# Fused attention, MoE and expert MoE: the experts' first pass in another order, and copies of MoE1's second product moved to ScalarE

## The chip, the core and the metric

The kernel runs on one core of a Trainium2 chip. Five engines run side by side, each with its own queue in program order: TensorE (PE; its weight loads are shown as PEld), VectorE (DVE), ScalarE (ACT), GpSimd (POOL) and SyncE (SP), which here only issues DMAs. GpSimd issues the indirect DMAs (gather and scatter by a list of rows) and ScalarE the stores of `y`. The metric is the device time of one execution in microseconds; lower is better.

## The reference

```python
attn_out = _attn_ref(q, k, v)                  # causal attention, 2 x 12 heads, 448 tokens, 64 wide
x = attn_out.transpose(0, 2, 1, 3).reshape(896, 768)
h = x @ w_in                                   # MoE1: 768 -> 2048
x = (h * (1 / (1 + exp(-1.702 * h)))) @ w_out  # 2048 -> 768
logits = x @ w_gate                            # MoE2: 8 experts, one per token
e_idx = argmax(logits, axis=1)
gate_w = softmax(logits)[e_idx]
eom = sigmoid(x @ w_output_gate)
for e in range(8):                             # 768 -> 1024 -> 768
    mask = e_idx == e
    out[mask] = gate_w[mask] * eom[mask, e] * (relu(x[mask] @ w1[e]) @ w2[e])
```

Everything is float32 to the outside.

## The kernel before

The kernel works with float32 products made of three: each operand is split into a high part (rounded, on ScalarE) and the rest (a subtraction, on VectorE or GpSimd), and TensorE adds high by high, high by rest and rest by high in PSUM. The order of all engines is written out by hand.

**Attention and MoE1's first product** take the first 246 us and are not touched.

**MoE1's second product** (`l2`) goes through the seven tiles of 128 tokens twice: first for the last 256 of the 768 columns (part "B"), then for the first 512 (part "A"). Within a tile it runs over 16 blocks of 128 rows of the weight (`kk`). Every fourth block it calls `gsplit`, which casts a piece of `g` on ScalarE (L505) and subtracts on GpSimd or VectorE (L507). After each block the weight stream is pumped: a weight tile is unpacked in three instructions on VectorE (L219, L221, L224), cast on ScalarE (L226) and subtracted on GpSimd (L228). At the end of a tile ScalarE copies the result out of PSUM (`y`, L597) and stores it. One tile behind, in hooks at given `kk`, the routing runs: `tr_y` transposes `y` on TensorE (L615) and copies the transposes to `yT` (L617), `logits` multiplies them with the gates (L627) and copies them out (L629, L632, L633); in part A follow `pick` (which expert, and the token's weight; L649 to L664) and `place` (the token's place in its expert's list, L670 to L677, and a scatter of token number and weight to the list in DRAM, L678).

**The experts** (`block`) are worked through in passes of up to 128 tokens; twelve passes run here, the first two both for expert 0. The first takes tokens of the first five tiles, so that it can start before the last tile is routed. A pass has twelve steps u. Steps 0 to 5 (`l1`, L875 and L879) multiply the tokens `xh`, `xl` with two blocks of `w1`; after steps 2 and 5 comes a relu on ScalarE (L883); `tr` transposes the hidden values (L889) and splits them into `hh`, `hl` (L891, L892). Steps 6 to 11 (`l2m`, L899 and L901) multiply with `w2`. After every step, `split` casts one later weight tile on ScalarE (L300) and subtracts on VectorE (L301), into one of six pairs `ent`; five tiles are split ahead during the last tile of part A. From split 12 on (counted from 0), each issues a load of the weights two passes ahead on SP's queue (`again`, `load32`, L272), which waits until the split has read its place; there are 24 places.

In the first pass, hooks `(hf, k)` between the matmuls of steps 0 to 5 and hooks `u` behind the later steps finish the routing of the last tile: `tr_y`, `logits`, `pick`, `place`, then `rest_lists` reads the rest of expert 0's list (`le0`, L724) and the other lists, `first_x` gathers its tokens into `xw` (L686) and `prep` transposes (L696) and splits (L698, L699) them for the second pass.

Of the kernel before, what the change touches and what calls it, by code (L numbers as in the profile page):

```python
# [9 lines left out]
F32 = mybir.dt.float32  # L10
# [97 lines left out]
def kernel(ctx, tc, q, k, v, w_in, w_out, w_gate, w_og, w1, w2, out):  # L108
    nc = tc.nc
# [3 lines left out]
    NE, _, F2 = w1.shape  # L113
# [7 lines left out]
    TT = NT // 128  # L121
# [25 lines left out]
    dram = ctx.enter_context(tc.tile_pool(name="dram", bufs=1, space=DRAM))  # L147
# [11 lines left out]
    with tc.manual_schedule():  # L159
# [90 lines left out]
        NR, NU, NENT = 24, 12, 6  # L250
# [23 lines left out]
        def again(o, u, last):  # L274


            if last and o + 2 < NE + 2:
                load32(o + 2, u)
# [13 lines left out]
        def split():  # L292
            if nsplit[0] == len(order):
                return
            p, u = order[nsplit[0]]
            hi, lo = entry_of[p, u] = entries[nsplit[0] % NENT]
            nsplit[0] += 1
            o, last = passes[p]
            raw = places[(NU * o + u) % NR]
            nc.scalar.copy(hi, raw)  # L300
            nc.vector.tensor_sub(lo, raw, hi.bitcast(F32))  # L301
            again(o, u, last)
# [155 lines left out]
        for s in range(len(steps) + LAG + AV_AT[-1]):  # L458
# [12 lines left out]
            for c in range(NKC):  # L471
                u = s - LAG - (NQ - 1) - AV_AT[c]
# [37 lines left out]
        for fq in range(4):  # L510
            for fc in range(4):
# [13 lines left out]
                if f == 15:  # L525
# [4 lines left out]
                    lgB = mp.tile([64, TT, 128], F32, name="lgB")  # L530
# [79 lines left out]
        def tr_y(t, part):  # L610
            n = 4 if part == "A" else 2
            y = ys_t.pop((t, part))
            p = ps.tile([128, 4, 128], F32, name="ps_yT", tag="tp", bufs=2)
            for c in range(n):
                nc.tensor.transpose(p[:, c], y[:, c * 128:(c + 1) * 128], ident)  # L615
            yT = mp.tile([128, 4, 128], F32, name="yT", tag="yT", bufs=1)
            nc.vector.tensor_copy(yT[:, :n], p[:, :n])  # L617
            yT_t[t, part] = yT

        lg_t = {}  # L620
# [1 line left out]
        def logits(t, part):  # L622
            n, k0 = (4, 0) if part == "A" else (2, 4)
            yT = yT_t.pop((t, part))
            p = ps.tile([128, 128], F32, name="ps_lT", tag="sm", bufs=2)
            for c in range(n):
                nc.tensor.matmul(p[32 * c:32 * c + 32], wg[:, k0 + c], yT[:, c], start=True, stop=True)  # L627
            if part == "B":
                nc.vector.tensor_copy(lgB[:, t], p[0:64])  # L629
            else:  # L630
                lT = mp.tile([128, 128], F32, name="lT", tag="lT", bufs=2)
                nc.vector.tensor_add(lT[0:64], p[0:64], lgB[:, t])  # L632
                nc.vector.tensor_copy(lT[64:128], p[64:128])  # L633
                lg_t[t] = lT

        def logits_sum(t):
            lg = ps.tile([128, 2 * NE], F32, name="ps_lg", tag="sm", bufs=2)
            nc.tensor.matmul(lg, lg_t.pop(t), esum, start=True, stop=True)
            lg_t[t] = lg

        ohs = {}

        def pick(t):
            logits_sum(t)
            lg = lg_t.pop(t)
            nm = mp.tile([128, 8], F32, name="nm", tag="nm", bufs=2)
            tmp = mp.tile([128, 3, NE], F32, name="tmp", tag="tmp", bufs=2)
            ohb = mp.tile([128, NE], BF16, name="ohb", tag="ohb", bufs=2)
            nc.vector.tensor_reduce(nm[:, 0:1], lg[:, 0:NE], axis=AX.X, op=ALU.max)  # L649
            nc.vector.scalar_tensor_tensor(tmp[:, 0], lg[:, 0:NE], nm[:, 0:1], rev,  # L650
                                           op0=ALU.is_equal, op1=ALU.mult)
            nc.vector.tensor_reduce(nm[:, 1:2], tmp[:, 0], axis=AX.X, op=ALU.max)
            nc.vector.tensor_scalar(ohb, rev, nm[:, 1:2], None, op0=ALU.is_equal)
            nc.vector.tensor_add(acc[t + 1], acc[t], ohb)
            nc.vector.tensor_scalar(nm[:, 2:3], nm[:, 0:1], -1.0, None, op0=ALU.mult)
            nc.scalar.activation(tmp[:, 1], lg[:, 0:NE], AF.Exp, bias=nm[:, 2:3], scale=1.0,
                                 accum_out=nm[:, 4:5])
            nc.vector.tensor_mul(tmp[:, 2], lg[:, NE:2 * NE], ohb)
            nc.vector.tensor_reduce(nm[:, 3:4], tmp[:, 2], axis=AX.X, op=ALU.add)
            nc.scalar.activation(nm[:, 5:6], nm[:, 3:4], AF.Exp, scale=-1.0)  # L660
            nc.vector.tensor_scalar_add(nm[:, 4:5], nm[:, 4:5], 1e-9)
            nc.vector.tensor_scalar_add(nm[:, 5:6], nm[:, 5:6], 1.0)
            nc.vector.tensor_mul(nm[:, 6:7], nm[:, 4:5], nm[:, 5:6])
            nc.vector.reciprocal(lst[:, t, 1:2], nm[:, 6:7])  # L664
            ohs[t] = ohb

        def place(t):
            ohb = ohs.pop(t)
            p = ps.tile([128, 2 * NE], F32, name="ps_rk", tag="sm", bufs=2)
            nc.tensor.matmul(p[:, 0:NE], sut, ohb, start=True, stop=False)  # L670
            nc.tensor.matmul(p[:, 0:NE], ones, acc[t], start=False, stop=True)
            tmp = mp.tile([128, NE], F32, name="tmp2", tag="tmp2", bufs=2)
            pos = mp.tile([128, 1], F32, name="pos", tag="pos", bufs=2)
            pos_i = mp.tile([128, 1], I32, name="pos_i", tag="pos_i", bufs=2)
            nc.vector.tensor_mul(tmp, p[:, 0:NE], ohb)
            nc.vector.tensor_reduce(pos, tmp, axis=AX.X, op=ALU.add)
            nc.vector.tensor_copy(pos_i, pos)  # L677
            nc.gpsimd.indirect_dma_start(  # L678
                out=xl_d[:, :], out_offset=bass.IndirectOffsetOnAxis(ap=pos_i.bitcast(U32), axis=0),
                in_=lst[:, t, :].bitcast(I32), in_offset=None, bounds_check=NT * NE - 1, oob_is_err=False)  # L680
# [4 lines left out]
        def gather(lw, xw, nrow=NT):  # L685
            nc.gpsimd.indirect_dma_start(  # L686
                out=xw, out_offset=None, in_=y1_d[0:nrow, :],
                in_offset=bass.IndirectOffsetOnAxis(ap=lw[:, 0:1].bitcast(U32), axis=0),
                bounds_check=nrow - 1, oob_is_err=False)

        def prep(xw):
            for hf in range(2):
                p = ps.tile([128, 4, 128], F32, name="ps_x", tag="tp", bufs=2)
                for c in range(3):
                    kk = 3 * hf + c
                    nc.tensor.transpose(p[:, c], xw[:, kk * 128:(kk + 1) * 128], ident)  # L696
                dst = xh[:, 3 * hf:3 * hf + 3]
                nc.scalar.copy(dst, p[:, 0:3])  # L698
                nc.vector.tensor_sub(xl[:, 3 * hf:3 * hf + 3], p[:, 0:3], dst.bitcast(F32))  # L699
# [30 lines left out]
        for t in range(TT):  # L730
            hooks = {}
# [6 lines left out]
        for t in range(TT):  # L738
# [13 lines left out]
            def h7(t=t):  # L752
                if t:
                    pick(t - 1)
# [13 lines left out]
            hooks = dict(zip(R_AT, (h2, h5, h7, h10, h15)))  # L768
# [7 lines left out]
        xw = xw_t[0]  # L776
# [78 lines left out]

        npass = [0]

        def block(lw, hooks):

            o, last = passes[npass[0]]  # L860
            p0 = npass[0]
# [4 lines left out]
            def hook(k):  # L866
                if k in hooks:
                    hooks[k]()
# [13 lines left out]
            def relu(hf):  # L882
                nc.scalar.activation(hs[:, hf * 512:(hf + 1) * 512], hps[hf], AF.Relu)  # L883
# [19 lines left out]
            for u in range(6):  # L903
                if u == 4:
                    tr(0)
                l1(u)
                if u % 3 == 2:
                    relu(u // 3)
                split()
            hook("b")  # L910
            pyA = ps.tile([128, 512], F32, name="ps_yA", tag="acc", bufs=4)
            pyB = ps.tile([128, 512], F32, name="ps_yB", tag="acc", bufs=4)
# [2 lines left out]
            for u in range(6, NU):  # L915
                g4, r = (u - 6) // 3 * 4, (u - 6) % 3
                if u == 7:
                    tr(1)
                if r < 2:
                    l2m(pyA, u, 512, range(g4 + 2 * r, g4 + 2 * r + 2))  # L920
                else:
                    l2m(pyB, u, 256, range(g4, g4 + 4))
                if u == 10:
                    nc.scalar.activation(ys[:, 0:512], pyA, AF.Copy, scale=scl)
                if u == 11:
                    nc.scalar.activation(ys[:, 512:768], pyB[:, 0:256], AF.Copy, scale=scl)
                split()
                hook(u)
            nc.gpsimd.indirect_dma_start(
                out=out[:, :], out_offset=bass.IndirectOffsetOnAxis(ap=lw[:, 0:1].bitcast(U32), axis=0),  # L930
# [2 lines left out]
        engs = (ET.PE, ET.DVE, ET.Pool, ET.Activation, ET.SP)  # L933
        lists = [lw0, le0] + [lwin[:, e] for e in ORDER[1:]] + lo_t

        def first_x():
            gather(le0, xw)

        block(lw0, {
            (0, 1): lambda: tr_y(TT - 1, "A"), (0, 2): last_logits, (0, 3): lambda: pick(TT - 1),  # L940
            (0, 5): last_place, (1, 0): rest_lists, (1, 3): first_x, (1, 4): counts, 6: further_constants,
            10: lambda: prep(xw)})
        nov = None

        def some(p):
# [65 lines left out]
```

## Time and profile before

| what | us |
|---|---|
| median of 3 runs | 633.17 |
| lowest and highest run | 633.08, 637.72 |
| the profiled execution | 635.76 |
| its span, first to last instruction | 634.0 |
| attention and MoE1's first product | 0 to 246 |
| second product, part B | 246 to about 307 |
| second product, part A | to about 394 |
| the experts' passes | 394 to 629 |

A line of the timeline holds the start, the time from the first to the last end of a run of equal instructions, the engine, the line of the kernel, the operation, output and input tile, the count, and in brackets how long the engine stood idle before and what it waited for. Instructions in a run overlap a little, so that a line's end is not always where the next begins.

### The profile page before, as it was taken

What the parts mean: (1) busy time and instruction counts of PE and PEld (TensorE: products, weight loads), DVE (VectorE), ACT (ScalarE), POOL (GpSimd) and SP (SyncE); (2) the same over time, 40 slices, a digit from 0 to 9 for tenths busy, and PEclk for the clock granted to TensorE, in tenths of its full rate; (3) what the DMA queues carried; (4) which work ended last, traced back from release to release, by engine and by line L of the source; (5) the groups of instructions that cost most, each with busy time, mean ns of one, the idle gap of its engine ahead of it and who ended that gap; (6) DMA issues with size and microseconds to landing.
All of it is one profiled execution on the core that took longest, in us unless ns stands there. A gap on an engine that the chain in (4) does not pass through costs nothing. (4 is left out here: it accounts for less than half of the span.)

```text
span 634.0 us, 10087 instructions
## 1 busy us (share of the span) xinstructions
PE 592.1 (93%) x3326; PEld 477.9 (75%) x3326; DVE 470.1 (74%) x890; ACT 372.1 (59%) x729; POOL 202.4 (32%) x291
## 2 busy tenths in 40 slices
PE   6999999999999979787999999959999999999995
PEld 4666666688888859687877777747888888888884
DVE  2767877467777786877844457839998888898896
ACT  3888888333333324434332225737888888888885
POOL 3354444334333343757400012230551111011110
PEclk8999999999999979998999999979999999999998
DMA  6835552125444443402592305148999999999950
GB/s 138 244 85 142 115 120 62 55 68 144 135 134 138 140 148 100 150 17 81 162 348 36 131 17 174 53 154 273 353 365 353 360 335 383 380 382 381 382 191 20
DMA packets 93144, 118.02 MB, mean 186 GB/s; under 512 B 40206, under 2 KB 53406, under 8 KB 93088
## 3 DMA queue, kind: packets, MB, share of 16 engines
q1 hardware_dynamic: 88560, 109.05, 53.3%
q0 software_dynamic: 2512, 5.54, 2.5%
q10 hardware_dynamic: 2016, 2.75, 1.2%
q8 instruction: 28, 0.46, 0.4%
q14 instruction: 28, 0.23, 0.1%
HBM read 114.10 MB, written 7.54 MB: 192 GB/s over the span
## 5 line engine op out<-in xcount | busy, mean ns | idle before, releaser
L575 PE MATMUL py<-slotA,gs 128*128 128x256 f32 (+1 forms) x609 | 115.2, 343 | 1.3 <-POOL gs L507 1.3
L575 PEld LDWEIGHTS py<-slotA,gs 128*128 128x128 f32 x609 | 93.4, 196 | 14.4 <-issue 2.7
L437 PE MATMUL ph<-xhi,slotA 128*128 128x512 f32 (+1 forms) x384 | 97.5, 373 | 4.7 <-DVE g L536 4.7
L228 POOL TENSOR_TENSOR slotA<-w,slotA 128x512 fp32r<-128x512 f32 x45 | 62.0, 1379 | 81.7 <-ACT slotA L226 81.6
L437 PEld LDWEIGHTS ph<-xhi,slotA 128*128 128x128 f32 x384 | 70.8, 191 | 15.3 <-issue 5.8
L226 ACT CAST slotA<-w 128x512 fp32r<-128x512 f32 x45 | 27.9, 620 | 89.9 <-DVE w L224 89.9
L301 DVE TENSOR_TENSOR ent<-wraw,ent 128x1024 fp32r<-128x1024 f32 x48 | 58.0, 1221 | 4.9 <-ACT ent L300 4.9
L437 PE MATMUL ph<-xlo,slotA 128*128 128x512 f32 x192 | 56.0, 372 | 0.0
L367 PE MATMUL sc<-kT,qz 128*128 128x64 f32 (+6 forms) x168 | 52.6, 397 | 3.0 <-ACT kT L358 2.8
L507 DVE TENSOR_TENSOR gs<-g,gs 128x512 fp32r<-128x512 f32 x38 | 31.5, 837 | 31.8 <-ACT gs L505 31.8
L390 POOL TENSOR_SCALAR P<-P,rc 128x64 f32<-128x64 f32 (+2 forms) x72 | 36.7, 511 | 54.4 <-DVE rc L389 40.5
L875 PE MATMUL ps_h<-ent,xh 128*128 128x512 f32 x192 | 53.9, 402 | 0.0
L224 DVE SCALAR_TENSOR_TENSOR w<-raw,w 128x512 uint32<-128x512 uint32 x46 | 51.9, 1129 | 1.2
L381 ACT ACTIVATE P<-sc,nmax 128x64 f32<-128x64 f32 (+6 forms) x84 | 40.3, 480 | 18.7 <-DVE nmax L379 7.6
L300 ACT CAST ent<-wraw 128x1024 fp32r<-128x1024 f32 x48 | 49.9, 1051 | 0.4 <-ACT y L597 0.4
L379 DVE TENSOR_REDUCE nmax<-sc 128x1 f32<-128x64 f32 (+6 forms) x84 | 34.6, 416 | 16.6 <-PE sc L368 16.4
L536 DVE TENSOR_TENSOR g<-ph,g 128x256 f32<-128x256 f32 x64 | 23.6, 389 | 30.1 <-ACT g L535 30.1
L505 ACT CAST gs<-g 128x512 fp32r<-128x512 f32 x56 | 33.1, 617 | 14.7 <-PE py L575 9.1
L875 PEld LDWEIGHTS ps_h<-ent,xh 128*128 128x128 f32 x192 | 35.0, 188 | 7.3
L398 PE MATMUL ps_pT<-ident,P 128*128 128x128 f32 x192 | 37.7, 289 | 2.2 <-POOL P L390 1.6
L301 DVE TENSOR_TENSOR ent<-wrb,ent 128x1024 fp32r<-128x1024 f32 x30 | 36.3, 1222 | 4.7 <-ACT ent L300 4.2
L221 DVE SCALAR_TENSOR_TENSOR w<-raw,w 128x512 uint32<-128x512 uint32 x46 | 38.0, 827 | 1.6
(190 smaller groups left out, 1211.8 us busy)
## 6 DMA issues: line engine op xcount, KB each, us to landing
wraw<-in_moe_w_dram SPq DMA_DIRECT2D x66, 512.0 KB, 7.8
wrb<-in_moe_w_dram SPq DMA_DIRECT2D x48, 512.0 KB, 8.2
wr<-in_moe_w_dram SPq DMA_DIRECT2D x30, 512.0 KB, 6.2
raw<-in_moe_w_in_dram SPq DMA_DIRECT2D x24, 512.0 KB, 4.3
raw<-in_moe_w_out_dram SPq DMA_DIRECT2D x22, 512.0 KB, 3.6
qraw<-in_q_dram SPq DMA_DIRECT2D x24, 112.0 KB, 2.9
kraw<-in_k_dram SPq DMA_DIRECT2D x24, 112.0 KB, 2.9
vraw<-in_v_dram SPq DMA_DIRECT2D x24, 96.0 KB, 2.5
```

What stands on the lines that cost most here:

```text
L221: nc.vector.scalar_tensor_tensor(wu, r[:, :, 1], 0xC0000000, wu, op0=ALU.bitwise_and, op1=ALU.bitwise_or)
L224: nc.vector.scalar_tensor_tensor(wu, r[:, :, 0], 29, wu, op0=ALU.logical_shift_right, op1=ALU.bitwise_or)
L228: nc.gpsimd.tensor_sub(slot[:, 1], w, slot[:, 0].bitcast(F32))
L300: nc.scalar.copy(hi, raw)
L301: nc.vector.tensor_sub(lo, raw, hi.bitcast(F32))
L367: nc.tensor.matmul(sc[:, :n], qT[:, j].rearrange("d h p -> d (h p)"), kT[:, :n], start=True, stop=False)
L381: nc.scalar.activation(Pb[j][:, :n], sc[:, :n], AF.Exp, bias=nm, scale=1.0, accum_out=sm)
L390: eng[NORM_ENG[j]].tensor_scalar(Pb[j][:, :n], Pb[j][:, :n], rc, 1.0, op0=ALU.mult, op1=ALU.mult)
L398: nc.tensor.transpose(ps[:, c].rearrange("p h q -> p (h q)"), Pb[j][:, c * KC:(c + 1) * KC], ident)
L437: nc.tensor.matmul(p[:, 0:128 * nt], wt, xt[:, kk, 128 * t0:128 * (t0 + nt)], start=kk == 0 and n == 0, stop=kk == KD - 1 and n == 2)
L575: nc.tensor.matmul(py[:, :n], gt[:, kk % 4], wt, start=kk == 0 and m == 0, stop=kk == KF - 1 and m == 2)
L875: nc.tensor.matmul(hps[hf], xh[:, k0 + n], wt[:, n], start=k0 + n == 0 and m == 0, stop=False)
```

## The change

Two things are changed. In `tr_y` and `logits`, the copies out of PSUM that VectorE made alone (all but the addition into `lT`) are made by ScalarE. In the first pass, no weight tile is split after steps 0, 1 and 2, two are split after each of steps 3, 4 and 5, and one after each later step, so that the count is the same from step 6 on; `pick` of the last tile leaves its second half (`weigh`, the token's weight) to `place`, which runs it behind its own three VectorE instructions and ahead of the scatter; behind the gather of the second pass's tokens SP gets a DMA of four bytes of `xw` to DRAM, which waits for the gather; and `prep` for the second pass comes after step 11, no longer after step 10.

```diff
@@ tr_y, logits
-            nc.vector.tensor_copy(yT[:, :n], p[:, :n])
+            nc.scalar.copy(yT[:, :n], p[:, :n])
...
-                nc.vector.tensor_copy(lgB[:, t], p[0:64])
+                nc.scalar.copy(lgB[:, t], p[0:64])
...
-                nc.vector.tensor_copy(lT[64:128], p[64:128])
+                nc.scalar.copy(lT[64:128], p[64:128])
@@ pick, place
-        def pick(t):
+        def pick(t, split_off=False):
...
+            if not split_off:
+                weigh(t, nm, tmp, lg, ohb)
+            else:
+                late_w.append((t, nm, tmp, lg, ohb))
+            ohs[t] = ohb
+
+        late_w = []
+
+        def weigh(t, nm, tmp, lg, ohb):
             nc.vector.tensor_mul(tmp[:, 2], lg[:, NE:2 * NE], ohb)
             nc.vector.tensor_reduce(nm[:, 3:4], tmp[:, 2], axis=AX.X, op=ALU.add)
             nc.scalar.activation(nm[:, 5:6], nm[:, 3:4], AF.Exp, scale=-1.0)
...
             nc.vector.tensor_copy(pos_i, pos)
+            while late_w:
+                weigh(*late_w.pop())
             nc.gpsimd.indirect_dma_start(
@@ block
-        def block(lw, hooks):
+        def block(lw, hooks, rate=(1,) * NU):
...
-                split()
+                for _ in range(rate[u]):
+                    split()
@@ the first pass
+        gate = dram.tile([1, 1], F32, name="gate")
+
         def first_x():
             gather(le0, xw)
+            nc.sync.dma_start(gate, xw[0:1, 0:1])
 
         block(lw0, {
-            (0, 1): lambda: tr_y(TT - 1, "A"), (0, 2): last_logits, (0, 3): lambda: pick(TT - 1),
+            (0, 1): lambda: tr_y(TT - 1, "A"), (0, 2): last_logits, (0, 3): lambda: pick(TT - 1, True),
             (0, 5): last_place, (1, 0): rest_lists, (1, 3): first_x, (1, 4): counts, 6: further_constants,
-            10: lambda: prep(xw)})
+            11: lambda: prep(xw)}, (0, 0, 0, 2, 2, 2, 1, 1, 1, 1, 1, 1))
```

## Rows read from the trace of the kernel before

**Rows 1.** Busy time by stage: from:to, length, each engine's busy us, clock, DMA, GB/s.

```profile
253.00:320.00 67.00, 56.67 (x390) 50.54 (x389) 51.50 (x59) 26.03 (x49) 40.34 (x28) 0.95 0.34 112
...
475.00:500.00 25.00, 25.00 (x144) 21.53 (x144) 22.06 (x24) 20.83 (x29) 2.54 (x2) 1.00 1.02 359
```

**Rows 2.** The same view, a short stretch behind the first pass's stall.

```profile
422.00:426.00 4.00, 4.00 (x19) 3.82 (x18) 1.12 (x2) 1.69 (x4) 0.00 (x0) 0.54 0.00 0
```

**Rows 3.** Timeline of TensorE, end of the first pass and start of the second.

```profile
409.25 1.11 PE L899 MATMUL ps_yB<-ent,hh 128*128 128x256 f32 x8
...
410.66 1.09 PE L899 MATMUL ps_yA<-ent,hh 128*128 128x512 f32 x4
...
421.10 1.51 PE L696 MATMUL ps_x<-ident,xw 128*128 128x128 f32 x6 [7.51 <-DMA xw<-y_d,le]
422.26 2.05 PE L899 MATMUL ps_yB<-ent,hh 128*128 128x256 f32 x8
...
424.97 1.40 PE L875 MATMUL ps_h<-entb,xh 128*128 128x512 f32 x4
```

**Rows 4.** Timeline of VectorE, first pass.

```profile
400.51 0.17 DVE L658 TENSOR_TENSOR tmp<-ps_lg,ohb 128x8 f32<-128x8 f32 x1 [0.48 <-ACT tmp L656]
...
402.08 1.23 DVE L301 TENSOR_TENSOR entb<-wraw,entb 128x1024 fp32r<-128x1024 f32 x1 [0.39 <-ACT entb L300]
...
410.85 2.35 DVE L301 TENSOR_TENSOR entb<-wr,entb 128x1024 fp32r<-128x1024 f32 x2
```

**Rows 5.** Timeline of GpSimd, first pass.

```profile
404.04 1.73 POOL L678 DMA_INDIRECT xl_d<-lst,pos_i  x1 [9.80 <-DVE pos_i L677]
...
409.36 1.90 POOL L724 DMA_INDIRECT le<-xl_d,ix  x1 [3.47 <-DMA xl_d<-lst,pos_i]
...
413.46 1.81 POOL L686 DMA_INDIRECT xw<-y_d,le  x1 [1.22 <-issue]
```

**Rows 6.** DMA issues, last number us to landing: gathers at 413.46, 386.52 and 611.53.

```profile
xw<-y_d,le POOLq DMA_INDIRECT x1, 7.5
...
xw<-y_d,lw POOLq DMA_INDIRECT x1, 4.6
...
xw<-y_d,lo POOLq DMA_INDIRECT x1, 2.1
```

**Rows 7.** Timeline of TensorE, second product: waits for `yT`.

```profile
268.77 0.64 PE L627 MATMUL ps_lT<-yT,wg 128*32 128x128 f32 x4 [2.34 <-DVE yT L617]
...
285.39 0.41 PE L627 MATMUL ps_lT<-yT,wg 128*32 128x128 f32 x4 [1.32 <-DVE yT L617]
...
295.86 0.60 PE L627 MATMUL ps_lT<-yT,wg 128*32 128x128 f32 x4 [3.66 <-DVE yT L617]
...
384.44 0.43 PE L627 MATMUL ps_lT<-yT,wg 128*32 128x128 f32 x8 [0.62 <-DVE yT L617]
```

**Rows 8.** Timeline of VectorE: the `yT` copies of two of these tiles.

```profile
284.92 0.42 DVE L617 COPY yT<-ps_yT 128x256 f32<-128x256 f32 x1
...
295.39 0.41 DVE L617 COPY yT<-ps_yT 128x256 f32<-128x256 f32 x1
```

**Rows 9.** Timeline of ScalarE: `gs` casts of these tiles, and two split casts.

```profile
285.56 1.66 ACT L505 CAST gs<-g 128x512 fp32r<-128x512 f32 x3
...
293.48 1.65 ACT L505 CAST gs<-g 128x512 fp32r<-128x512 f32 x3
...
602.25 2.01 ACT L300 CAST entb<-wr 128x1024 fp32r<-128x1024 f32 x2
```

**Rows 10.** The copies by line: count, shortest, median and longest in ns, forms.

```profile
L597 ACT COPY y<-py x14: 362/481/606, 255.4 to 394.1; 128x256 f32<-128x256 f32 x7, 128x512 f32<-128x512 f32 x7
...
L617 DVE COPY yT<-ps_yT x14: 411/550/690, 257.2 to 396.1; 128x256 f32<-128x256 f32 x7, 128x512 f32<-128x512 f32 x7
```

**Rows 11.** Timeline of SyncE: loads of weights, first five and five late ones.

```profile
412.09 16.24 SPq L272 DMA_DIRECT2D wr<-in_moe_w_dram  x5
...
568.74 6.93 SPq L272 DMA_DIRECT2D wr<-in_moe_w_dram  x5
```

More of the change, by code (lines that the diff above doesn't have):

```diff
@@ L664, in pick @@
             nc.vector.reciprocal(lst[:, t, 1:2], nm[:, 6:7])
-            ohs[t] = ohb
         def place(t):
@@ L926, in block @@
                     nc.scalar.activation(ys[:, 512:768], pyB[:, 0:256], AF.Copy, scale=scl)
-                split()
+                for _ in range(rate[u]):
+                    split()
                 hook(u)
```

## The prediction

> **What bounds the kernel now.** I read the stages first (busy time by window). In the experts' passes from the second on TensorE is busy all the time: 25.00 of 25.00 us, beside DMA engines at 1.02 [rows 1]. Nothing in this change touches a step of such a pass, so it can only win where TensorE stands still ahead of them. Two such places are large. In the first part of MoE1's second product (253 to 320 us, part "B", 256 columns) TensorE is busy for 56.67 of 67.00 us [rows 1]: 10.3 us idle. In the experts' first pass (`p0 = 0`) it stands for 7.51 us on the gather of the next tokens, between the steps u=10 and u=11 [rows 3].
>
> The second stall also slows the clock: the granted share is 0.54 between 422 and 426 us [rows 2], the lower of the two levels (1.2 instead of 2.4 GHz) for most of it, right after TensorE had been idle. The same eight matmuls of `l2m` that take 1.11 us at 409.25 take 2.05 at 422.26, and the six transposes take 1.51 [rows 3].
>
> Then the chain before that stall, engine by engine. On VectorE the last tile's `pick` and `place` are in pieces: 0.48 us idle for ScalarE's exponential, then 0.39 us idle for the cast of an early split, then that split's 1.23 us subtraction; only behind it come the three instructions of `place` [rows 4]. GpSimd, which waited for the last of them (`pos_i`), then writes the list (404.04), reads its part back (409.36) and gathers (413.46) [rows 5]. The gather lands 7.5 us after its issue [rows 6], which is when TensorE goes on.
>
> **The first pass, step by step.** Times are on the axis of the profile before.
>
> (1) With no split in u=0 to 2, the split's idle time and its subtraction (0.39 + 1.14, since the next instruction starts 1.14 us later) leave the chain, and `weigh`, moved behind `place`'s three instructions, has its exponential ready: the 0.48 goes too [rows 4]. The scatter still waits for `weigh`, since it sends the weight as well. Together 2.0 us: scatter at 402.0, and with the same steps between, gather at 411.4 instead of 413.46 [rows 5]. `lT`'s second half on ScalarE beside its first on VectorE could add 0.3; I leave it out.
>
> (2) The gate: a 4-byte DMA on SP's queue that waits for the gathered tokens. Queued behind it are the loads that splits 12 and later set off, five of them between 412 and 428 us now [rows 11]; who waits for those comes below. So the gather runs alone. No row shows this very gather alone. The nearest are 2.1 us (the last one, when the loads have ended) and 4.6 us (the first pass's own, loads beginning halfway) [rows 6]. I take 3.5, between the two: no load beside it, as with the last one, but more tokens. It lands at 414.9 (413.5 to 416.0).
>
> (3) What TensorE does until then. The late splits are now VectorE's queue: split 5 can't be subtracted before about 402.7 (`weigh`'s exponential keeps ScalarE until 401.1, and a relu of 0.6, by the copies of its shape [rows 10], and a cast of 1.0 [rows 9] lie ahead). Up to the second half of `hl`, which is queued behind them, stand seven subtractions at 1.14 [rows 4], two `hl` at about 0.65 (an estimate: half a split's columns) and 0.3 of `counts`: 9.6 us, so `hl` is whole at 412.2. TensorE, whose transposes wait for a relu that no longer has a split's cast of 1.0 us ahead of it [rows 9], reaches u=9 some 0.8 us before the 410.66 of today [rows 3], wants `hl` 0.9 us later and waits about 1.5 us. Then u=9's rest, u=10 and u=11 at 1.4 us each [rows 3] end at 415.5. The gather has landed: the 7.51 us stall is gone, and 1.5 us has come in its place.
>
> (4) `prep` moved from hook 10 to 11: u=11 no longer waits, but the transposes are now bare, and on ScalarE the `ys` activation and the cast of split 16 come before the casts of `xh`: 415.7 + 0.5 + 1.0 + 0.5 = 417.7, the second pass's first matmul. It starts at 424.97 now [rows 3]. `xl` stands behind split 16 on VectorE (about 0.4 us lost in that step), and the step no longer runs at the lower clock (1.40 for four matmuls; 0.3 won). Gain of the pass: 7.2 us.
>
> **MoE1's second product.** Fourteen `yT` copies leave VectorE (median 0.55 us, 7.7 us in all); on ScalarE the same two shapes out of PSUM take 0.36 and 0.61 [rows 10]. The logits' copies are smaller than any of these. What matters is the order. In part B the waits for `yT` stop TensorE for 2.34, 1.32 and 3.66 us in three tiles [rows 7]. VectorE's and ScalarE's queues hold each other: ScalarE's cast of a weight slot waits for VectorE's unpacking (L224), the `gs` cast stands behind it, VectorE's subtraction L507 waits for that, and `yT` stood behind L507. On ScalarE `yT` follows the `gs` cast directly. In the tile at 295.86: the cast ends at 294.1, so `yT` is there at 294.5 and not at 295.8: 1.3 us earlier [rows 7 to 9]. The tile at 268.77 is of the same kind (1.6). The tile at 285.39 goes the other way: `yT` follows L224 directly on VectorE (284.92), but on ScalarE stands behind the slot's cast and the `gs` cast (until 286.1) [rows 8, 9]: 0.7 to 1.2 us later. Since VectorE loses 0.41 us of `yT` and a smaller copy per tile [rows 10], each tile also begins a little earlier. Carrying the three tiles on, TensorE reaches the second part 1.7 us earlier; bounds: 0 (the later tiles give it all back) and 4 (nearly all that six tiles take off VectorE lies on the path).
>
> In part A nine matmuls stand between a tile's transposes and its logits, over 2 us of work, so copies there are hidden (without that cover 0.6 each). Only that tile waits, 0.62 us, behind a split's subtraction [rows 7]; on ScalarE only the cast is ahead: 0.6 gained.
>
> The Trainium skill (ScalarE: Activation LUTs, "Rules for kernel authors") says to give plain arithmetic to VectorE, since that is the faster engine per element. The trace doesn't bear that out for a float32 copy out of PSUM of these shapes. By the rule the copies would be a loss of some tenths of a microsecond each, and the sum 1 to 2 us smaller.
>
> **Sum.** 7.2 + 1.7 + 0.6 = 9.5 us. The profiled execution took 635.76 us (span 634.0); from that, 626.3. The median of the runs is 633.17, 2.6 below the profiled one; the gain is the same: **623.7 us**.
>
> **Rivals.** (a) The gather is slow by itself, and the hold brings nothing: 7.5 us from 411.4 lands at 418.9. TensorE idles 3.4 us, the clock falls again as in [rows 2], and about 3.2 of the 7.2 are left: 5.5 in all, 627.7 us. For it: the gather's own GpSimd time is 1.81 [rows 5]. Against it: the 2.1 and 4.6 us landings [rows 6]. The Trainium skill (DMA: Bandwidth & Descriptors, "Queues, rings and completion order") has each DMA engine take turns between queues packet by packet, which would leave the gather half of the bandwidth next to any number of loads and so gain little from holding them. That is this rival; 2.1 against 7.5 us speaks against it.
>
> (b) The other side: ScalarE's queue holds `yT` back in most tiles as at 285.39. Such a tile's wait grows from 1.32 to 3.0 by my replay and the clock falls behind it (at 295.86, after 3.66 us idle, four small matmuls take 0.60 where 0.41 is normal [rows 7]; about 1.0 us a tile, by the 0.94 that eight matmuls lose in [rows 3]): 2.7 us a tile. Three such tiles give back the 7.8 that the rest wins; four make it 3.0 us slower, 636.2. One or two: 628 to 631. For it: it does happen in one tile. Against it: in the two tiles with the longest waits VectorE's L507 stands ahead of `yT` [rows 8].
>
> (c) The held loads come late for the passes. Loads start at 415 instead of 412 while the passes start 7.3 us sooner: 10 us of lead lost. The lead is long: a load issued at 568.74 [rows 11] is first read at 602.25 [rows 9]; if it lands in the 7.5 us that the gather takes among loads [rows 6], it is 26 us early. Were the DMA engines unable to keep up, the passes would be paced by them and the gain gone: 633.
>
> **Chances.** Forecast 0.66, its own range 620.5 to 626.5 (gather bounds cost nothing up to a landing at 416.6; part B 0 to 4; 1 us for VectorE's queue). (a) 0.13; (b) one or two tiles 0.10, more 0.05; (c) 0.04; the rest unforeseen. The range for 8 in 10 reaches to (a): 619.5 to 628.5. About 1% (6.3 us) is what a measurement of this kernel can tell from no change. Faster by more takes a gain over 6.3: nearly all of the forecast and a part of (a) and (b), 0.73; within 1%: the rest of (a), one or two tiles of (b), half of (c), 0.20; slower 0.07.
>
> **What would show it.** After: scatter to gather about 9.4 us as now; the gather landing in 2 to 5 us with no weight load beside it, the first load right behind it; no stall on `xw` above 1 us; a wait of 1 to 2 us for `hl` near u=9; the second pass starting about 7 us sooner relative to the first. Part B's `yT` waits under 5 us in all. It would be wrong if the gather still takes 7 us, if a part-B tile waits over 3 us for `yT`, or if a pass of 18.2 us grows.

## The result and the profile after

The changed kernel takes 627.70 us (median of four executions, 627.14 to 628.88) beside 633.78 us of the kernel before (median of four, 633.08 to 637.72). The ratio over the runs is 0.988, with a 95% interval of 0.985 to 0.992: faster by 0.8 to 1.5%. (The two medians divided give 0.990.) The profiled execution took 627.73 us, its span is 626.0 instead of 634.0.

The experts' first pass, by windows (columns as in [rows 1]; the second line lies over the same stretch as the stage in [rows 1]):

```profile
394.00:432.00 38.00, 34.38 (x183) 26.79 (x182) 30.33 (x52) 28.39 (x39) 9.27 (x27) 1.00 0.54 180
...
253.00:320.00 67.00, 57.14 (x396) 50.42 (x395) 48.63 (x45) 29.89 (x65) 40.85 (x28) 0.97 0.36 116
```

In the first line TensorE stands still for 3.6 of 38 us and its clock is at 1.00 throughout; before, the 7.51 us stall alone lay in this stretch and the clock fell behind it [rows 2, 3]. In part B of the second product (second line) TensorE is busy only 0.5 us more than before [rows 1], while VectorE has 2.9 us less to do.

TensorE's timeline in the first pass after:

```profile
391.97 1.20 PE L885 MATMUL ps_h<-entb,xh 128*128 128x512 f32 x4 [0.24 <-ACT xh L708]
...
410.43 0.74 PE L911 MATMUL ps_yA<-ent,hl 128*128 128x512 f32 x2 [1.22 <-DVE hl L902]
...
413.80 0.82 PE L706 MATMUL ps_x<-ident,xw 128*128 128x128 f32 x6
415.95 1.20 PE L885 MATMUL ps_h<-entb,xh 128*128 128x512 f32 x4 [1.33 <-ACT xh L708]
```

The stall on the gather [rows 3] is gone: the transposes of `xw` at 413.80 wait for nothing. In its place stand two shorter waits: 1.22 us for `hl`, which VectorE makes behind its splits, and 1.33 us for `xh`, which ScalarE casts behind a split. From the first pass's first matmul (391.97; 393.92 before) to the second's (415.95; 424.97 before, [rows 3]) it takes 23.98 us instead of 31.05.

GpSimd's chain (scatter, list, gather), the four-byte DMA on SyncE's queue ("the gate") with the loads behind it, and the two instructions of ScalarE that TensorE waits for at the end:

```profile
400.26 0.99 POOL L688 DMA_INDIRECT xl_d<-lst,pos_i  x1 [6.65 <-DVE lst L673]
404.50 1.38 POOL L734 DMA_INDIRECT le<-xl_d,ix  x1 [3.12 <-DMA xl_d<-lst,pos_i]
...
408.89 1.81 POOL L696 DMA_INDIRECT xw<-y_d,le  x1 [2.03 <-PE ps_yB L911]
```

```profile
413.42 0.31 SPq L952 DMA_DIRECT2D gate<-xw  x1
413.83 3.34 SPq L272 DMA_DIRECT2D wr<-in_moe_w_dram  x5
```

```profile
414.47 1.04 ACT L300 CAST ent<-wr 128x1024 fp32r<-128x1024 f32 x1
415.41 0.87 ACT L708 CAST xh<-ps_x 128x384 fp32r<-128x384 f32 x2
```

The gather is issued 16.9 us after the pass began (19.5 before: 413.46 - 393.92, [rows 3, 5]) and the gate goes off 4.5 us after the gather's issue. `xh` is cast only behind split 16 (414.47).

TensorE in part B, the waits that answer to [rows 7]:

```profile
267.12 0.41 PE L627 MATMUL ps_lT<-yT,wg 128*32 128x128 f32 x4 [0.54 <-ACT yT L617]
...
273.40 0.44 PE L615 MATMUL ps_yT<-ident,y 128*128 128x128 f32 x2 [2.09 <-ACT y L597]
...
286.41 0.64 PE L627 MATMUL ps_lT<-yT,wg 128*32 128x128 f32 x4 [2.74 <-ACT yT L617]
...
294.32 0.41 PE L627 MATMUL ps_lT<-yT,wg 128*32 128x128 f32 x4
...
299.63 0.44 PE L615 MATMUL ps_yT<-ident,y 128*128 128x128 f32 x2 [1.11 <-ACT y L597]
```

The waits of 2.34 and 3.66 us became 0.54 and none, the one of 1.32 became 2.74, and new waits, now for `y` itself, have come up.

### The profile page after: what moved, and what is told of

It is laid out like the page before. It is cut to its first block, busy times and chain, and to the rows that moved or that the text cites. A ratio compares the mean times of both kernels' runs of the same rounds, so it can differ in the third digit from the quotient of the medians.

```text
span 626.0 us, 10088 instructions
## 1 busy us (share of the span) xinstructions
PE 590.1 (94%) x3326; PEld 474.5 (76%) x3326; DVE 460.3 (74%) x862; ACT 380.7 (61%) x757; POOL 200.5 (32%) x291
## 5 line engine op out<-in xcount | busy, mean ns | idle before, releaser
L575 PEld LDWEIGHTS py<-slotA,gs 128*128 128x128 f32 x609 | 92.1, 192 | 15.1 <-issue 2.8
```

The source lines that it names most:

```text
L575: nc.tensor.matmul(py[:, :n], gt[:, kk % 4], wt, start=kk == 0 and m == 0, stop=kk == KF - 1 and m == 2)
```

## The experiments

Two lengths, each read from one trace, compare the kernels without the start of the program, which shifts from run to run: "up to the pass" is the time from TensorE's first transposes of `y` (L615, near 256 us) to the first pass's first matmul; "the pass" is from there to the second pass's first matmul. Ratios are to the kernel before, with their 95% intervals. How far one trace can be trusted: the kernel before gives the same lengths twice to 0.04 and 0.19 us, but kernels that have the same second product as the changed one reach the pass in 136.0 to 136.1 us six times and in 136.6 to 136.7 twice.

| kernel | us (median) | before beside it | ratio | up to the pass | the pass |
|---|---|---|---|---|---|
| before | | | | 138.14 | 31.05 |
| before again | 636.3 (one, profiled) | 633.49 | | 138.18 | 31.24 |
| changed | 627.70 | 633.78 | 0.988 (0.985 to 0.992) | 136.01 | 23.98 |
| pass alone | 629.44 | 634.29 | 0.992 (0.989 to 0.995) | 138.15 | 23.73 |
| copies alone | 632.97 | 634.29 | 0.999 (0.997 to 1.000) | 136.64 | 29.68 |
| no hold | 627.76 | 634.29 | 0.989 (0.987 to 0.992) | 136.07 | 23.94 |
| early splits | 629.83 | 634.29 | 0.994 (0.992 to 0.996) | 136.02 | 25.84 |
| prep after step 10 | 627.25 | 633.49 | 0.989 (0.988 to 0.991) | 136.05 | 23.77 |
| weigh undone | 627.46 | 633.11 | 0.992 (0.990 to 0.994) | 136.08 | 23.62 |
| hold alone (with copies) | 630.98 | 633.11 | 0.997 (0.995 to 0.998) | 136.06 | 28.07 |
| fewer splits at the end | 625.36 | 633.49 | 0.987 (0.985 to 0.989) | 136.67 | 21.89 |
| slot's cast later | 622.82 | 633.49 | 0.982 (0.980 to 0.984) | 131.99 | 23.97 |
| both of these | 620.98 | 633.11 | 0.982 (0.980 to 0.984) | 131.96 | 21.88 |
| both, prep after step 10 | 623.48 | 633.11 | 0.985 (0.984 to 0.987) | 132.01 | 25.38 |

### Pass alone and copies alone

The first takes the three copies back to VectorE, the second makes only those three lines of the change in the kernel before.

```diff
-            nc.scalar.copy(yT[:, :n], p[:, :n])
+            nc.vector.tensor_copy(yT[:, :n], p[:, :n])
...
-                nc.scalar.copy(lgB[:, t], p[0:64])
+                nc.vector.tensor_copy(lgB[:, t], p[0:64])
...
-                nc.scalar.copy(lT[64:128], p[64:128])
+                nc.vector.tensor_copy(lT[64:128], p[64:128])
```

> The first pass's new order alone; the copies stay on VectorE. If the two parts add up: the second product is as before (waits for yT of 2.3, 1.3 and 3.7 us, first pass starting near 394), the first pass takes about 24.3 us from its start to the second pass's instead of 31.05 before and 23.98 with both, and the time lies about 2 us above that of the changed kernel, near 629.7. Rival: the copies bring nothing in the whole, 627.7. Rival: the copies are needed for the pass, whose list comes too late without them (lT on VectorE alone): the pass takes over 26 us, time over 631.

> The copies to ScalarE alone; the first pass in the old order. If the parts add up: first pass starting near 392.0, 1.9 us earlier than before; the pass itself near 31 us with the stall on the gather of 7 us; time about 2 us under before, 631 to 632. Rival: the copies move only waits about in part B (yT's wait to y's wait), and the gain at the first pass's start is under 0.7 us: 633.

The parts add up. The new pass alone takes 23.73 us and leaves the second product at 138.15; the copies alone bring the second product to 136.64 and leave the stall on the gather, in this execution 5.12 us:

```profile
418.43 1.51 PE L696 MATMUL ps_x<-ident,xw 128*128 128x128 f32 x6 [5.12 <-DMA xw<-y_d,le]
```

So the pass is the larger part (ratio 0.992 against 0.999). By the medians the pass alone wins 4.9 us and the copies alone 1.3, together 6.2 beside the 6.1 of the changed kernel; the trace gives the pass 7.3, beside a profile of the kernel before that lies above its median (below). The copies' interval reaches past 1.000, so the times alone don't show that they gain; the 1.5 to 2.1 us are read from the trace, and 632.97 misses the expected 631 to 632.

Inside the first pass the copies don't help. With them and the old order the scatter is issued 11.4 us after the pass began, 10.1 before; with the new order it is 8.3 with them and 8.0 without.

### No hold, and hold alone

The first takes the four-byte DMA out of the changed kernel. The second keeps it, with the copies, and puts everything else in the first pass back.

```diff
@@ no hold
             gather(le0, xw)
-            nc.sync.dma_start(gate, xw[0:1, 0:1])
@@ hold alone
-            ... (0, 3): lambda: pick(TT - 1, True),
+            ... (0, 3): lambda: pick(TT - 1),
...
-            11: lambda: prep(xw)}, (0, 0, 0, 2, 2, 2, 1, 1, 1, 1, 1, 1))
+            10: lambda: prep(xw)})
```

> The changed kernel without the four-byte DMA, so that weight loads start when their place is read. Theory: the gather is now issued so much earlier (2.5 us before the first load may start, at 411.4) that only its last rows meet loads; it lands 1 to 3 us later than 413.3 and the second pass starts 0 to 1.5 us later, since the cast of xh waits for other work until 415.4 anyway: 627.7 to 629.2. Rival: the hold is what makes the gather fast; without it it takes 7.5 us again and lands at 416.4, TensorE idles 2.6 us and its clock falls: 3 to 4 us, 631 to 632.

> The copies and the hold, with the pass otherwise in the old order: one split after every step, the weight computed in pick, prep after step 10. It tells whether the hold does in the old order what it did not do in the new. Theory: the hold and the earlier gather stand in for each other; here the gather is issued as late as before (19.5 us after the pass begins), meets no loads, lands in 4.5 to 5 us instead of 6.1 to 7.8, and the pass takes 27 to 28.5 us instead of 29.7 to 31.2. Rival: loads never slowed the gather; landing 6 to 7.5 and a pass of 29.5 or more.

Without the hold nothing is lost: 23.94 us for the pass, 627.76 in all, at the lower end of what was expected. Its gather (GpSimd), its landing (DMA issues) and its first load (SyncE):

```profile
410.14 1.70 POOL L696 DMA_INDIRECT xw<-y_d,le  x1 [2.15 <-PE ps_yB L911]
```

```profile
xw<-y_d,le POOLq DMA_INDIRECT x1, 4.3
```

```profile
412.67 5.62 SPq L272 DMA_DIRECT2D wr<-in_moe_w_dram  x5
```

The first load sets out 2.5 us after the gather, which lands in 4.3 us all the same. In the old order it is the other way round: there the first load goes out 1.4 us ahead of the gather [rows 5, 11], which then takes 7.5 us [rows 6] (copies alone: 6.1). And there the hold helps: with it the gather, issued at 411.84 and no earlier in the pass than before, lands in 4.5 us, and the pass takes 28.07 us instead of the 29.68 of the copies alone.

```profile
416.43 1.51 PE L706 MATMUL ps_x<-ident,xw 128*128 128x128 f32 x6 [3.56 <-DMA xw<-y_d,le]
```

So loads do slow this gather, when they are ahead of it: it lands in 6.1 to 7.8 us in the three traces in which a load is (the third is the second profile of the kernel before), and in 3.5 to 4.7 us in all the others. The hold and the earlier gather stand in for each other: with the gather early, the hold is worth nothing. That the hold wins 1.6 us in the old order rests on one trace of either kernel; the ratios, 0.997 and 0.999, point the same way, but their intervals overlap.

### Early splits, prep after step 10, weigh undone

Each puts one thing of the new pass back: the rates to one split after every step, `prep` to hook 10, the token's weight into `pick`.

```diff
@@ early splits
-            11: lambda: prep(xw)}, (0, 0, 0, 2, 2, 2, 1, 1, 1, 1, 1, 1))
+            11: lambda: prep(xw)})
@@ prep after step 10
-            11: lambda: prep(xw)}, ...
+            10: lambda: prep(xw)}, ...
@@ weigh undone
-            ... (0, 3): lambda: pick(TT - 1, True),
+            ... (0, 3): lambda: pick(TT - 1),
```

> The changed kernel with one split after every step again, as before; hold, weigh and prep stay moved. Theory: the gather comes 1.5 to 2 us later, but hl is no longer late at step 9 (1.2 us won) and split 16's cast is earlier, so that the second pass starts only 0.3 to 1 us later: 628 to 628.7. Rival: the splits' order is a full term of the gain, as the prediction has it (2.0 us): 629.7 or more.

> The changed kernel with prep after step 10 again. Theory: the gather lands near 413.3 and step 10 ends at 412.4, so TensorE waits about 1 us there, but step 11 then covers the casts of xh, which no longer stand behind split 16: second pass starting between 0.5 us earlier and 0.5 us later, 627.2 to 628.2. Rival: any wait ahead of step 11 costs as before, with the clock falling: 1.5 us or more later, 629.2 and up.

> The changed kernel with the token's weight computed in pick again, ahead of place. Theory: the list comes 0.5 us later and so does the gather, but its landing is not what the second pass waits for (the cast of xh behind split 16 is): the pass stays at 24.0 us within 0.3, 627.7. Rival: the chain to the gather is still the bound: 0.5 us or more.

The splits' order is worth 1.9 us (25.84 against 23.98). I had expected a third of it; in size the rival came out (629.83 beside its "629.7 or more"). The gather comes 2.8 us later in the pass (19.7 against 16.9), yet TensorE waits only 0.68 us for it. TensorE's timeline with early splits, and ScalarE's, show where the rest goes:

```profile
397.89 0.40 PE L638 MATMUL ps_lg<-esum,lT 128*128 128x16 f32 x2 [1.14 <-ACT lT L633]
...
403.63 0.66 PE L899 MATMUL ps_hT<-ident,hs 128*128 128x128 f32 x4 [2.30 <-ACT hs L893]
```

```profile
397.58 0.26 ACT L633 COPY lT<-ps_lT 64x128 f32<-64x128 f32 x1 [1.48 <-DVE lT L632]
...
402.89 0.20 ACT L669 ACTIVATE nm<-nm 128x1 f32<-128x1 f32 x1 [2.02 <-DVE nm L668]
403.00 0.58 ACT L893 ACTIVATE hs<-ps_h 128x512 f32<-128x512 f32 x1
```

`lT`'s half on ScalarE waits for the half on VectorE (L632), which stands behind a split's subtraction there. The relu (L893) waits behind `weigh`'s exponential (L669), which waits for VectorE, and that is busy with a split. So TensorE loses 3.4 us early in the pass and 0.7 on the gather, and wins back the 1.2 us for `hl` and 0.8 of the wait for `xh`.

The other two moves are worth nothing that can be told. `prep` after step 10 makes TensorE wait 1.12 us for the gather, and step 11 then hides the casts; the pass takes 23.77 us. With `weigh` back in `pick` it takes 23.62. There the list does not come 0.5 us later, as I had expected: the scatter is issued 8.4 us after the pass began, 8.3 in the changed kernel.

```profile
414.56 0.85 PE L706 MATMUL ps_x<-ident,xw 128*128 128x128 f32 x6 [1.12 <-DMA xw<-y_d,le]
416.66 1.09 PE L885 MATMUL ps_h<-entb,xh 128*128 128x512 f32 x4
```

### The kernel before, once more

> The kernel before, once more, for a second profile. The profiled execution (635.76) was 2.0 to 2.6 us above the median of its runs. Theory: the excess lies in the first pass's stall on the gather and the clock behind it, which differ from run to run. Rival: it lies elsewhere (attention, the end), and this one shows the same stall to 0.3 us.

It shows the same pass, with the same stall to 0.3 us, and took 636.3 us beside a median of 633.49:

```profile
421.55 1.51 PE L696 MATMUL ps_x<-ident,xw 128*128 128x128 f32 x6 [7.80 <-DMA xw<-y_d,le]
```

So the stall is no accident of one profile. That is what the rival expected to see, but it doesn't show where the excess lies. Both profiled executions lie 2.0 to 2.8 us above the median of the runs beside them; those of the other kernels lie between 0.8 us below and 1.1 us above theirs. Of the 39 other executions of the kernel before, two lay as high (636.2 and 637.72). That the shorter ones had a shorter stall would fit, and in the copies alone the same stall is 5.12 us; but no trace of such an execution exists, and it stays open.

### Two variants that gain

Both start from the changed kernel. One takes away what holds the first pass now: a split fewer ahead of the second `hl` and one fewer at the end, made up behind the second pass's first step. The other is for part B: ScalarE's cast of a weight slot moves one pump step later, next to GpSimd's subtraction, so that it no longer stands in ScalarE's queue while VectorE unpacks.

```diff
@@ fewer splits at the end
-            11: lambda: prep(xw)}, (0, 0, 0, 2, 2, 2, 1, 1, 1, 1, 1, 1))
+            11: lambda: prep(xw)}, (0, 0, 0, 2, 2, 1, 1, 1, 1, 1, 1, 0))
...
-            block(lists[p], hooks)
+            block(lists[p], hooks, (3,) + (1,) * (NU - 1) if p == 1 else (1,) * NU)
@@ slot's cast later (st.late is set ahead of the second product)
                 nc.vector.scalar_tensor_tensor(wu, r[:, :, 0], 29, wu,
                                                op0=ALU.logical_shift_right, op1=ALU.bitwise_or)
-                nc.scalar.copy(slot[:, 0], w)
-                yield
+                if not st.late:
+                    nc.scalar.copy(slot[:, 0], w)
+                    yield
+                else:
+                    yield
+                    nc.scalar.copy(slot[:, 0], w)
                 nc.gpsimd.tensor_sub(slot[:, 1], w, slot[:, 0].bitcast(F32))
```

> The changed kernel with one split fewer ahead of the first pass's second hl and one fewer at its end; both are made up behind the second pass's first step (rates 0,0,0,2,2,1,1,1,1,1,1,0, then 3,1,...). Theory: what holds the first pass now is VectorE's and ScalarE's queue of splits: hl comes 1.1 us earlier (its wait of 1.22 us nearly gone), the cast of xh is no longer behind split 16 (1 us): second pass starting 1.5 to 2 us earlier, 625.7 to 626.5, if the second pass's wait for hl (0.59 us) doesn't grow. Rival: the second pass pays the splits back: same time as the changed kernel, 627.7. Rival: the gather's landing (413.3) is the bound already: under 1 us won.

> The changed kernel with ScalarE's cast of a weight slot in the second product one pump step later (with GpSimd's subtraction), so that ScalarE's queue does not stand still for VectorE's unpacking. Theory: part B's waits for y and yT (4.5 and 3.3 us) come from ScalarE standing behind that cast; they shrink to under 3 us in all and the first pass starts 2 to 5 us earlier: 623 to 626. Rival: VectorE's own chain (unpacking and the subtractions of gs) is the bound of part B; the waits turn up at gs, under 1 us won: 627.

> The two variants that gained, together: the slot's cast one pump step later in the second product, and the first pass's last splits made up in the second pass. They act in different stages; if they add up: first pass 4.0 us earlier, the pass 2.1 us shorter, 620.5 to 621. Rival: an earlier first pass meets DMA traffic of the second product's end and the pass gives back 1 us or more.

> The same with prep after step 10. Step 10 ends 1.2 us sooner than in the changed kernel while the gather lands when it did, so TensorE should wait 2 us or more there, and the clock may fall: 0.5 to 2 us slower than the variant with prep after step 11. Rival: step 11 covering the casts is worth as much as the wait: same time.

Fewer splits: the wait for `hl` is gone, the one for `xh` is 0.39 instead of 1.33 us, and the pass takes 21.89:

```profile
412.84 0.82 PE L706 MATMUL ps_x<-ident,xw 128*128 128x128 f32 x6
414.04 1.20 PE L885 MATMUL ps_h<-entb,xh 128*128 128x512 f32 x4 [0.39 <-ACT xh L708]
```

The slot's cast later: no wait for `yT` is left in part B, those for `y` come to 2.9 us instead of 4.5, and TensorE is busy for 61.31 us of the same 67 (57.14 in the changed kernel), although no work was taken off any engine. Windows and waits of this variant:

```profile
253.00:320.00 67.00, 61.31 (x429) 53.17 (x428) 53.16 (x52) 30.54 (x66) 42.91 (x29) 1.00 0.41 140
```

```profile
PE ps_yT L620 <- ACT y L602: 2.9, 5, 0.7
```

Together they give both gains in full (131.96 and 21.88) and 620.98 us, the fastest here: 0.982 of the kernel before. With `prep` after step 10 that kernel waits 2.42 us for the gather, the granted clock falls to 0.50 right behind the wait, the lower of the two levels (1.2 of 2.4 GHz), and the pass is 3.5 us longer (the time 2.5, more than the 0.5 to 2 expected): what was even in the changed kernel is now a loss. TensorE's timeline and the window behind the wait:

```profile
408.31 1.51 PE L711 MATMUL ps_x<-ident,xw 128*128 128x128 f32 x6 [2.42 <-DMA xw<-y_d,le]
409.47 2.06 PE L915 MATMUL ps_yB<-ent,hh 128*128 128x256 f32 x8
```

```profile
408.00:410.00 2.00, 1.69 (x8) 1.72 (x9) 1.08 (x2) 0.62 (x2) 0.00 (x0) 0.50 0.12 42
```

## Why the prediction was right or wrong

The time, 627.7, lies inside the stated range (619.5 to 628.5) and outside the forecast's own (620.5 to 626.5). The direction and the place were right; 9.5 us were predicted, and between the two profiled executions it is 8.0, between the medians 6.1. That 627.7 is also the number of rival (a), whose mechanism did not come, is chance; without (a) the range would not have reached so far.

**The first pass's length (7.2) was right between the profiles: 7.07.** By the medians the new pass is worth 4.9. Steps (3) and (4) hold nearly to the row. `hl` makes step 9 wait 1.22 us (1.5 predicted), and the second pass waits behind split 16's cast for `xh`. The second pass's first matmul was put at 417.7 on the axis of the profile before, which is 415.4 when the predicted 2.3 us ahead of the pass are taken off; it came at 415.95.

**Step (1), the chain, was right in size and wrong in its parts.** The gather is issued 2.6 us earlier in the pass (2.0 and a possible 0.3 predicted). Of these the scatter comes 1.8 earlier; 0.8 lie between scatter and gather (8.6 us, 9.4 before), which I had held fixed. The 0.48 us that moving `weigh` was to win are not there: in place of the exponential, VectorE waits 0.38 us for `place`'s matmul (second line below), and with the move undone the scatter comes 0.1 us later.

```profile
395.90 0.26 ACT L633 COPY lT<-ps_lT 64x128 f32<-64x128 f32 x1 [0.86 <-DVE lT L632]
...
398.35 0.17 DVE L683 TENSOR_TENSOR tmp<-ps_rk,ohb 128x8 f32<-128x8 f32 x1 [0.38 <-PE ps_rk L679]
```

The possible 0.3 for `lT` has the wrong sign: ScalarE's half waits for VectorE's (first line), so the two run one behind the other, and with the copies on VectorE the gather is issued 0.3 us earlier in the pass. Of the waits of TensorE that the splits' order takes away, the sum had 0.8 us in step (3), the relu ahead of the transposes; in the changed kernel they come to 3.4.

**Step (2), the hold, was credited with what the order did.** The landing was inside its bounds, at their upper end (4.5 us at the gate; 3.5 taken, 2.1 to 4.6 the bounds), but the cause was not the hold: without it the gather lands in 4.3. The step that failed is that "So the gather runs alone" follows from the gate: the gather comes 2.5 us ahead of the first load, and no hold is needed. I had moved the gather to 411.4 in step (1), read the first load at 412.09 [rows 11], and did not put the two beside each other. They would have shown the gather 0.7 us ahead; the rest comes from the load, which the new order sends 1.4 us later in the pass, and from the gather's further 0.6.

**Step (4)**, `prep` behind step 11, was counted as a part of the way to 417.7 without an alternative; it is worth nothing either way (23.77 with hook 10). With it in the old place the passes behind are even 0.7 us shorter in its one trace, from the second pass's start to the last pass's `prep` 198.01 us against 198.75.

**MoE1's second product (1.7 and 0.6) was right: 2.1 in all.** The prediction's replay came out tile by tile: 1.6 us earlier was predicted at 268.77 (it is 1.65), 0.7 to 1.2 later at 285.39 (1.02), 1.3 earlier at 295.86 (1.54). In the copies alone and in the variant with fewer splits, whose second product is the same, the gain is 1.5 instead. The middle tile is rival (b) at work, once, as the replay had it. ScalarE's timeline there, with the copy behind the slot's cast, which waited 3.83 us for VectorE's unpacking, and the `gs` cast:

```profile
284.95 0.62 ACT L226 CAST slotA<-w 128x512 fp32r<-128x512 f32 x1 [3.83 <-DVE w L224]
285.48 0.61 ACT L505 CAST gs<-g 128x512 fp32r<-128x512 f32 x1
286.00 0.36 ACT L617 COPY yT<-ps_yT 128x256 f32<-128x256 f32 x1
```

That the slot's cast at the head of ScalarE's queue is the larger fault, the variant shows: moving it wins 4.0 us on top of the copies, twice what moving the copies won. What it would win with the copies left on VectorE was not run.

The rule of the Trainium skill to use VectorE for plain arithmetic (ScalarE: Activation LUTs, "Rules for kernel authors") gives its advantage for bf16; it is not borne out for these float32 copies out of PSUM: on ScalarE they take 0.36 and 0.59 us, on VectorE 0.41 and 0.69 [rows 10].

```profile
L617 ACT COPY yT<-ps_yT x14: 363/474/588, 257.4 to 394.5; 128x256 f32<-128x256 f32 x7, 128x512 f32<-128x512 f32 x7
```

**What was missing in the sum.** From 9.2 us at the start of the second pass (2.13 + 7.07) the 8.0 between the profiles follows by three small things: 0.3 lost in the passes, 0.7 between the last pass's `prep` and the end of the span, 0.2 in the start of the program. The last step, "the gain is the same", is what failed by most, 1.9 of the 3.4 us that are missing: it carried a difference of profiles over to medians, although the profiled execution was known to lie 2.6 us above its median. A second profile of that kernel shows the same pass and the same excess; what makes it is open.

**The rivals.** (a), a gather slow by itself, is refuted: without loads ahead it lands in 3.5 to 4.7 us, with them in 6.1 to 7.8. The page that speaks for it (the Trainium skill, DMA: Bandwidth & Descriptors, "Queues, rings and completion order", turns between queues by packets) is not contradicted by that, since a load ahead of the gather cost 1.6 to 3.3 us (over the 4.5 with the hold) and not more; but taking turns does not make it free. (c) did not come: TensorE waits for no load, and the passes behind take 198.75 us instead of 198.45.

## What to carry to other kernels

Before crediting a hold, put the two issue times beside each other: here the gather that was issued 2.5 us ahead of the loads needed no protection, and the one issued 0.4 to 1.4 us behind the first of them did. In queues that run in order, look at what stands at the head and waits: moving that one kind of instruction a step later won twice what moving the copies to another engine did. When a wait is taken out of a chain, look at what the chain waits for next: in place of the 0.48 us for `weigh`'s exponential came 0.38 for a matmul. And a gain read from two profiles is a gain between profiles; if the profiled execution lies off its median, the sum is uncertain by as much.

## What the runs showed of the hardware

The lower clock comes behind short stalls too. Behind TensorE's 2.42 us stall the granted clock is 0.50, behind the 2.74 us wait in part B of the changed kernel 0.57 (first line below). Behind a wait of 1.12 us with `prep` after step 10 it stays at 1.00 (second line), and so it does behind the 2.30 us wait with early splits (1.00 from 403.6 to 405.6).

```profile
286.00:288.00 2.00, 1.59 (x8) 1.21 (x9) 1.09 (x2) 1.66 (x5) 1.83 (x2) 0.57 0.71 246
...
415.00:417.00 2.00, 2.00 (x18) 1.96 (x17) 1.87 (x3) 1.11 (x4) 0.00 (x0) 1.00 0.45 124
```

Behind the stalls of 2.42, 3.56, 5.12 and 7.51 us the six transposes take the same 1.51 us (0.81 to 0.85 elsewhere) and the eight matmuls of step 11 about 2.06 instead of 1.1. From the transposes to the second pass's first matmul it is 3.52, 3.64, 3.60 and 3.87 us: a stall of 2.4 us pays nearly the same surcharge at this place as one three times as long.

The start of the program shifts by up to 1.6 us between executions of the same instructions (in the kernels that leave the slot's cast alone, TensorE's first transposes of `y` begin between 255.48 and 257.08); that is why the table compares lengths inside the trace.
